# A Fourier layer with a mixture of experts on one core: transposes partly on TensorE, routing by other VectorE steps, first loads on three queues, second products in halves

## The chip, the cores and the metric

The kernel runs on one core of one Trainium2 chip. The metric is the time of one execution in microseconds, as the device reports it; the median of several runs is compared. TensorE (PE) multiplies matrices, VectorE (DVE), ScalarE (ACT) and GpSimd (POOL) work element by element, and SyncE (SP) issues most of the DMA transfers. Every engine takes its instructions in the order in which the program lists them.

## The reference

```python
X = np.fft.rfft(x, axis=1)                      # x: 8 batches x 2496 x 256
Yr = Xr @ w_r - Xi @ w_i + b_r                  # 256 x 256 weights
Yi = Xr @ w_i + Xi @ w_r + b_i
Yr = sign(Yr) * max(abs(Yr) - 0.01, 0); Yi likewise
y = np.fft.irfft(Yr + 1j * Yi, n=2496, axis=1)  # 19968 tokens x 256
logits = y @ w_gate                             # 8 experts
e_idx = argmax(logits); gate_w = softmax(logits)[e_idx]
eom = sigmoid(y @ w_output_gate)
for e in range(8):                              # tokens of expert e
    out[mask] = gate_w * eom[:, e] * (relu(y[mask] @ w1[e]) @ w2[e])   # 256 -> 1024 -> 256
```

## The kernel before, in words

2496 is split as 39 x 64. The transform of a batch goes through these stages, each a set of matmuls on pairs of float16 tiles (a high and a low half of each number, three products for one).

- `load_x` brings a batch's `x` in six tiles; `scales` takes its largest magnitude, by squares on ScalarE or a maximum on VectorE, spreads it over the partitions with a matmul (`allmax`, line 394, whose operand `dg` comes from line 390) and makes the batch's scale `sx` of it.
- `stage1_pair` (line 588) multiplies by the 39-point table; ScalarE (597) and VectorE (598) take the two halves out of PSUM into `at`. There are eight PSUM banks in all.
- `load_a` (613) turns `at` round, 10 pieces `A` a batch of eight blocks of 128 x 128, each piece one transposing DMA on SyncE's queue.
- `stage2` (640) multiplies `A` with the table `ct`; lines 651, 652, 654 and 655 evict the result to `xt`. `mix` (664, 670) applies the weights, lines 685 to 690 the threshold, and line 700 the table `gt`; lines 714 to 717 evict to `bt` and `ste`.
- `inverse` transposes `bt` into `bdt` by DMA (739); `stage4` (765) makes `y`, which goes over `yt` (769) to DRAM as `yd` (785). `logits`, `gate` and `rank` compute each token's expert and its place among the expert's tokens.

Beside this, `weights` turns the expert weights into float16 pairs in DRAM (`wd`).

The tokens are then sorted into tiles of 128 of one expert. `routing` does it twice: phase 0 for the first four batches (64 tiles, placed in pairs), while later batches are still transformed, and phase 1 for all others (99 tiles). `blocks` finds each token's tile; three VectorE steps build, for four columns at a time, 0/1 matrices `ol` and `ob` (1135, 1136) and scale `ob` by the token numbers (1155); the matmul of line 1163 adds them into a map in PSUM; `indices` reads the map out.

For each tile `gathers` fetches the tokens (1236), `tokens` splits and transposes them (1255, 1256, 1269), `up` makes the first products (1354) which are evicted to `hh` (1364, 1365), and `down` the second ones (1325), evicted to `o` (1336) and scattered to the output (1339). `fetch` (1222) loads a tile's expert weights into one of three buffers `wbuf` in two parts, and only where the expert changes.

The order on every engine is set by `Issue`, a planner that runs while the program is built: generators ask for an engine with a due time and a duration, and the earliest due request whose resources are free is taken. The constants at the head of the file are its due times and durations. The first loads stand ahead of it, in the order of the code.

```python
        yield "A", r - SA, 0.66, lambda: A.activation(hi, pv[:, :, :, :m], AF.Copy, scale=sx)
        yield "D", r - SA, 0.68, lambda: V.scalar_tensor_tensor(lo, pv[:, :, :, :m], sx, hi, ALU.mult, ALU.subtract)
```

## Time and profile before

| | |
|---|---|
| median of three runs | 1507.56 us (1501.02 to 1515.1) |
| profiled execution | 1500.14 us, of which the span is 1498.4 us |
| mean granted clock of TensorE | 0.983 |
| busy: TensorE, VectorE, ScalarE, GpSimd | 1420.1, 970.0, 717.4, 590.9 us |
| instructions | 42257 |

The span runs from the first to the last instruction of the program. Busy time of an engine is the time in which at least one of its instructions ran; matmuls overlap each other, and the ends of matmuls are modelled. A line number is that of the listing. The granted clock is a share of 2.4 GHz; a matmul runs at half speed where it is 0.5.

### The profile page before, as it was taken

The numbers are of one execution on the slowest core, as the hardware profiler recorded it, in microseconds if no ns is written. First come the engines' busy times: TensorE is split into PE (matmuls) and PEld (weight loads), VectorE is DVE, ScalarE is ACT, GpSimd is POOL, SyncE is SP. The second block draws the span as 40 slices with busy tenths as digits, with TensorE's granted clock in tenths as the row PEclk, the third lists the DMA queues.
The fourth block names the chain that finished last, engine by engine and source line by source line (L and its number), as shares of the span: only waits on it lengthen the run. The fifth ranks groups of instructions, "written<-read, shape, count | busy, mean of one in ns | idle before, by whom it ended". The sixth has DMA issues, their size and how long they took to land. (4 is left out here: it accounts for less than half of the span.)

```text
span 1498.4 us, 42257 instructions
## 1 busy us (share of the span) xinstructions
PE 1420.1 (95%) x16192; PEld 1280.4 (85%) x16192; DVE 970.0 (65%) x2911; ACT 717.4 (48%) x1386; POOL 590.9 (39%) x664
## 2 busy tenths in 40 slices
PE   4799999998989989999999999999999999999998
PEld 4689887887778867878999988999898989999997
DVE  3677777769988878677777685555454555454532
ACT  4666765767665746343333333433333333333432
POOL 0454535444455545334333324344243333433311
PEclk8799999999999999999999999999999999999999
DMA  8879999999989898988865788765938476477420
GB/s 227 198 164 212 217 225 198 218 221 214 215 209 209 205 223 202 208 241 231 239 185 147 213 227 218 220 208 123 233 80 234 106 208 220 98 235 212 102 51 20
DMA packets 329955, 285.33 MB, mean 190 GB/s; under 512 B 277702, under 2 KB 286536, under 8 KB 317721
## 3 DMA queue, kind: packets, MB, share of 16 engines
q1 hardware_dynamic: 313127, 239.40, 65.4%
q0 software_dynamic: 15648, 42.17, 10.5%
q8 instruction: 127, 2.08, 0.6%
q10 hardware_dynamic: 978, 1.06, 0.3%
q14 instruction: 75, 0.61, 0.1%
HBM read 337.41 MB, written 58.91 MB: 264 GB/s over the span
## 5 line engine op out<-in xcount | busy, mean ns | idle before, releaser
L1354 PE MATMUL ps<-eT,wbuf 128*128 128x128 f16 (+1 forms) x6288 | 451.9, 232 | 5.6 <-DMA wbuf<-wd 4.3
L1325 PE MATMUL ps<-wbuf,hh 128*128 128x256 f16 x3912 | 444.8, 273 | 8.9 <-DVE hh L1365 4.0
L1354 PEld LDWEIGHTS <-wbuf 128*128 128x128 f16 x6288 | 419.7, 98 | 26.0 <-DMA wbuf<-wd 5.2
L1325 PEld LDWEIGHTS <-hh 128*128 128x128 f16 x3912 | 379.5, 98 | 57.0 <-DVE hh L1365 6.5
L1339 POOL DMA_INDIRECT out<-o,sidx x163 | 167.4, 1027 | 494.0 <-ACT o L1336 270.7
L1365 DVE SCALAR_TENSOR_TENSOR hh<-ps,hh 128x512 f16<-128x512 f32 x326 | 220.3, 689 | 206.7 <-ACT hh L1364 195.3
L1364 ACT ACTIVATE hh<-ps 128x512 f16<-128x512 f32 x326 | 188.3, 596 | 194.1 <-PE ps L1354 176.7
L670 PE MATMUL ps<-whl,xt 128*128 128x256 f16 x1920 | 229.3, 276 | 3.8 <-ACT xt L655 1.7
L670 PEld LDWEIGHTS <-xt 128*128 128x128 f16 x1920 | 190.2, 99 | 40.8 <-ACT xt L655 2.5
L1236 POOL DMA_INDIRECT yg<-yd,gidx x163 | 161.2, 989 | 93.2 <-DVE p2e L366 35.4
L1256 DVE SCALAR_TENSOR_TENSOR yhl<-yg,ys,yhl 128x256 f16<-128x256 f32 x163 | 79.6, 488 | 145.1 <-ACT yhl L1255 135.6
L1336 ACT ACTIVATE o<-ps,fac 128x256 f32<-128x256 f32 x163 | 76.8, 471 | 200.0 <-PE ps L1325 168.4
L1255 ACT ACTIVATE yhl<-yg,ys 128x256 f16<-128x256 f32 x163 | 82.2, 505 | 160.6 <-DMA eT<-yhl 78.1
L588 PE MATMUL ps<-f1t,x 117*128 117x120 f32 (+1 forms) x704 | 91.3, 291 | 6.1 <-issue 4.9
L588 PEld LDWEIGHTS ps<-f1t,x 117*128 117x128 f32 (+1 forms) x704 | 88.7, 207 | 7.4 <-issue 5.0
L689 POOL CAST zhl<-z 128x512 f16<-128x512 f32 x44 | 28.4, 647 | 139.1 <-DVE z L686 70.8
L765 PE MATMUL ps<-bdt,f4t 120*117 120x512 f16 x264 | 70.4, 390 | 10.5 <-ACT ste L716 8.5
L700 PE MATMUL ps<-gt,zhl 128*128 128x128 f16 x960 | 65.3, 220 | 9.9 <-DVE zhl L690 3.9
L700 PEld LDWEIGHTS <-zhl 128*128 128x128 f16 x960 | 58.1, 98 | 17.4 <-DVE zhl L690 4.4
L597 ACT ACTIVATE at<-ps,sx 128x480 f16<-128x480 f32 (+1 forms) x88 | 55.3, 649 | 34.2 <-PE ps L588 31.5
L685 ACT ACTIVATE zhl<-ps,sc 128x512 f32<-128x512 f32 x80 | 54.7, 687 | 32.9 <-PE ps L670 28.2
L690 POOL TENSOR_TENSOR zhl<-z,zhl 128x512 f16<-128x512 f32 x51 | 60.6, 1188 | 24.8 <-ACT zhl L688 21.4
(187 smaller groups left out, 1610.5 us busy)
## 6 DMA issues: line engine op xcount, KB each, us to landing
wbuf<-wd SPq DMA_DIRECT2D x262, 1024.0 KB
yd<-yt SPq DMA_DIRECT2D x120, 158.4 KB
x<-in_x SPq DMA_DIRECT2D x120, 156.0 KB
wr<-in_moe_w SPq DMA_DIRECT2D x32, 512.0 KB
wd<-wsp SPq DMA_DIRECT2D x64, 256.0 KB
yg<-yd,gidx POOLq DMA_INDIRECT x163
eT<-yhl SPq DMA_TRANSPOSE x163
out<-o,sidx POOLq DMA_INDIRECT x163
```

What stands on the lines that cost most here:

```text
L588: T.matmul(pv[:, dh, :, m * j:m * j + m], xs[:k, j0 + j, 128 * dh:128 * dh + 128], fw, start=True, stop=True)
L670: T.matmul(yp[:, 256 * j:256 * j + 256], xt_[:, v, 2 * dh + j, 64 - 64 * u:192 - 64 * u], whl[:, dh, vw, 256 * u:256 * u + 256], start=Fal ...
L700: T.matmul(bv[:, j], zhl[:, vz, c:c + 128], gt[:, 2 * p + j, v], start=(n == 0), stop=(n == 2))
L1236: yield "G", r + 5.6 * t - 30, 1.0, lambda: G.indirect_dma_start(out=yg, out_offset=None, in_=src, in_offset=bass.IndirectOffsetOnAxis(ap= ...
L1255: yield "A", r - 10, 0.5, lambda: A.activation(yhl[:, 0], yg[:, :256], AF.Copy, scale=s)
L1256: yield "D", r - 10, 0.48, lambda: V.scalar_tensor_tensor(yhl[:, 1], yg[:, :256], s, yhl[:, 0], ALU.mult, ALU.subtract)
L1325: T.matmul(pt[:, :256], hh[:, v, fc, 128 * n:128 * n + 128], w[:, fc // 2, vw, fc % 2], start=(k == 0), stop=(k == 23))
L1336: yield "A", r - 4, 0.47, lambda: A.activation(o, pt[:, :256], AF.Copy, scale=fac)
L1339: yield "G", r - 4, 1.0, lambda: G.indirect_dma_start(out=out, out_offset=bass.IndirectOffsetOnAxis(ap=sidx[:, t:t + 1], axis=0), in_=o, i ...
L1354: T.matmul(pt[:, 128 * m * j:128 * m * (j + 1)], w[:, dh, g // 4, vw, 128 * (g % 4):128 * (g % 4) + 128], eT[:, :m, v, dh], start=(n == 0) ...
L1364: yield "A", r, 0.6, lambda: A.activation(hv[:, 0], pt, AF.Relu)
L1365: yield "D", r, 0.69, lambda: V.scalar_tensor_tensor(hv[:, 1], pt, 0.0, hv[:, 0], ALU.max, ALU.subtract)
```

## The change

- Six of batch 0's ten `A` pieces, and four of every other batch's, are transposed by matmuls with an identity (`turn_a`) into PSUM and taken from there by ScalarE or VectorE, whichever the planner finds free first.
- `x` of batch 0 is issued by SyncE and ScalarE in turns, the biases and mixing weights by GpSimd; `m16` is loaded in two parts, `ct` and `gt` in two halves each, and what is not needed at once is given to the planner with a later due time.
- Routing: for each column one step over 128 elements makes `ol` and one step with two operations makes the scaled `ob`; the tables are float32 columns, and `ol` and `ob` are stored column by column. `blocks` treats two batches in a step and `indices` four.
- The second products of a tile are made in two halves, each as soon as its part of `hh` is ready, with due times between those of the first products.
- The constants of the planner are other ones; a line or two stands here for all.

```diff
-P = 69.05
-DK = 2.49
+P = 68.49
+TP, TE, QT = 0.56, -1.96, 6.13
+PT = (0, 1, 2, 3, 6, 8), (0, 1, 3, 6)
+DK = 2.8
...
-    for i in range(3):
-        load_x(0, i)
+    for i in range(6):
+        load_x(0, i, (nc.sync, nc.scalar)[i % 2])
...
-    nc.scalar.dma_start(wraw[:, :, 0], w_r.rearrange("(dh p) f -> p dh f", p=128))
+    G.dma_start(wraw[:, :, 0], w_r.rearrange("(dh p) f -> p dh f", p=128))
...
+    def tables_(r):
+
+        for i in range(2):
+            k = slice(K1 // 2 * i, K1 // 2 * (i + 1))
+            n = K1 // 2 * 256
+            yield from move(r, 6.5e5, 0.4, lambda: nc.sync.dma_start(ct[:, k].rearrange("p a b f -> p (a b f)"), cmat[:, n * i:n * (i + 1)]))
+            io.at(io.now + TAIL, io.set, "ct", i)
...
         for p in range(NP):
             yield slots["A"]
             a = st[b, "A", p] = ring(pm, [128, KP, 2, 2, 128], F16, "A", AN)
+            if p in PT[b > 0]:
+                for k in range(KP):
+                    io.go(turn_a(b, p, k, a, r + 2 * DK * p + TP))
+                continue
...
+    def turn_a(b, p, k, a, r):
+
+        def f(i):
+            pt = bank(i)
+            for dh in range(2):
+                for v in range(2):
+                    m = 256 * dh + 128 * v
+                    T.matmul(pt[:, m:m + 128], at[:, KP * p + k, dh, v], eye, start=True, stop=True)
+            return pt.rearrange("p (c v n) -> p c v n", c=2, v=2)
+
+        i, pt = yield "P", r, 0.23, f, True
+        yield [("A", r - TE, 0.58, lambda: A.activation(a[:, k], pt, AF.Copy)),
+               ("D", r - TE + QT, 0.68, lambda: V.tensor_copy(a[:, k], pt))]
...
-                ol = ring(pool, [P3, 128, CB], F16, f"ol{ph}", OL[ph])
-                ob = ring(pool, [P3, n, CB], F16, f"ob{ph}", OL[ph])
...
-                yield "D", r, 0.08 + 0.085 * m, lambda: V.tensor_tensor(ol[:, :, :m], iota[:P3, :, :m], bc(rlo, 128), ALU.is_equal)
-                yield "D", r, 0.08 + 0.066 * m, lambda: V.tensor_tensor(ob[:, :, :m], iota[:P3, :n, :m], bc(blk, n), ALU.is_equal)
+                ol = ring(pool, [P3, CB, 128], F16, f"ol{ph}", OL[ph])
+                ob = ring(pool, [P3, CB, n], F16, f"ob{ph}", OL[ph])
...
+                    for j in range(m):
+                        V.tensor_scalar(ol[:, j], iota[:P3], rlo[:, c0 + j:c0 + j + 1], None, ALU.is_equal)
...
+                    for j in range(m):
+                        V.tensor_scalar(ob[:, j], iota[:P3, :n], blk[:, c0 + j:c0 + j + 1], va[:, c0 + j:c0 + j + 1], ALU.is_equal, ALU.mult)
...
-        yield "D", r, 0.08 + 0.066 * m, lambda: V.tensor_tensor(ob[:, :, :m], ob[:, :, :m], vb, ALU.mult)
...
         for half in range(2 * m):
-            io.go(up(t, m, half, w, eT, ie, hh, r))
-        yield "hh", t
-        yield "w", t, 1
+            io.go(up(t, m, half, w, eT, ie, hh, r + UP * half))
...
-            io.go(down(t + i, m, i, w, hh, ih, r + 4 * m))
+            io.go(down(t + i, m, i, w, hh, ih, r + (5.6 + UP * i) * m + DN))
...
+        for half in range(2):
+            for i in range(m * half, m * half + m):
+                yield "hh", t0, i
+            if half == 0:
+                yield "P", r, 1.31, f, True
+            else:
+                yield "P", r + UP, 1.31, f
```

VectorE at the start, before: `mx` holds a batch's maxima, `x_211` is the first tile of the second batch, line 598 evicts the low halves of the first batch.

```order
L527 TENSOR_SCALAR sc_230<-sxi_240,swi 128x1
L359 TENSOR_REDUCE mx_242<-x_211 117x1
L598 SCALAR_TENSOR_TENSOR at<-ps_164,sx_238,at 128x40x12
L598 SCALAR_TENSOR_TENSOR at<-ps_171,sx_238,at 128x40x12
L598 SCALAR_TENSOR_TENSOR at<-ps_178,sx_238,at 128x40x12
```

The same place now, from the last evictions on (line 628 was 598, line 666 takes a transposed piece from PSUM).

```order
L628 SCALAR_TENSOR_TENSOR at<-ps_270,sx_236,at 128x40x12
L628 SCALAR_TENSOR_TENSOR at<-ps_283,sx_236,at 128x40x12
L491 SCALAR_TENSOR_TENSOR whl<-wr_112,sw,whl 128x2x512
L628 SCALAR_TENSOR_TENSOR at<-ps_290,sx_236,at 128x40x8
L519 MEMSET mx_262 128x12
L666 CAST A_313<-ps_318 128x512
```

The maximum over the second batch's first tile stood before the first eviction; now no maximum of that batch stands among the eleven evictions, and the transposed pieces follow them.

TensorE at the start, before: the last pairs of the first stage, three `allmax` products (of the gate weights and of the second batch), then the second stage.

```order
L588 MATMUL ps_280<-f1t,x_110 128x20x6 x4
L588 MATMUL ps_291<-f1t,x_110 128x20x6 x4
L588 MATMUL ps_299<-f1t,x_114 128x20x4 x4
L394 MATMUL ps_328<-dg_326,one_84 128x128
L394 MATMUL ps_356<-dg_354,one_84 128x128
L394 MATMUL ps_361<-dg_358,one_84 128x128
L640 LDWEIGHTS A_321
```

The same place now; line 661 is the transposing matmul, 32 of which follow before line 696, the second stage.

```order
L618 MATMUL ps_270<-f1t,x_104 128x20x6 x4
L618 MATMUL ps_283<-f1t,x_104 128x20x6 x4
L618 MATMUL ps_290<-f1t,x_108 128x20x4 x4
L661 LDWEIGHTS at
L661 MATMUL ps_318<-t_82,at 128x128
```

The three `allmax` products no longer stand between the two stages; transposing matmuls do.

ScalarE in the expert stage, before: line 1364 evicts half of a tile's first products, line 1336 a tile's second product, line 1255 splits gathered tokens.

```order
L1364 ACTIVATE hh_9453<-ps_25482 128x512
L1364 ACTIVATE hh_9453<-ps_25515 128x512
L1364 ACTIVATE hh_9602<-ps_25544 128x512
L1364 ACTIVATE hh_9602<-ps_25590 128x512
L1336 ACTIVATE o_25684<-ps_25618,fac_24244 128x256
L1255 ACTIVATE yhl_25648<-yg_24992,ys_25654 128x256
L1255 ACTIVATE yhl_25709<-yg_25052,ys_25719 128x256
L1336 ACTIVATE o_25752<-ps_25659,fac_24427 128x256
```

The same now (1458 was 1364, 1340 was 1255, 1430 was 1336).

```order
L1458 ACTIVATE hh_10068<-ps_26117 128x512
L1340 ACTIVATE yhl_26183<-yg_25505,ys_26215 128x256
L1458 ACTIVATE hh_10068<-ps_26186 128x512
L1430 ACTIVATE o_26264<-ps_26167,fac_24840 128x256
L1458 ACTIVATE hh_10068<-ps_26239 128x512
```

Two tiles went through together, four evictions of first products and then two second products; now each tile goes by itself, with one second product between the first products.

## Rows read from the trace of the kernel before

**Rows 1.** Page, busy microseconds of each engine, share of the span, instructions.

```profile
PE 1420.1 (95%) x16192; PEld 1280.4 (85%) x16192; DVE 970.0 (65%) x2911; ACT 717.4 (48%) x1386; POOL 590.9 (39%) x664
```

**Rows 2.** Stretches: length, busy of PE, PEld, DVE, ACT, POOL, clock, DMA share, GB/s.

```profile
0.00:52.00 52.00, 25.47 (x139) 23.50 (x140) 24.45 (x86) 23.62 (x43) 5.64 (x15) 0.75 0.89 224
52.00:350.00 298.00, 288.75 (x3214) 255.34 (x3213) 214.02 (x511) 199.44 (x379) 144.59 (x178) 0.99 0.96 206
350.00:600.00 250.00, 228.45 (x2473) 193.64 (x2471) 215.38 (x607) 161.40 (x321) 126.81 (x156) 0.97 0.93 211
600.00:700.00 100.00, 97.36 (x920) 83.70 (x919) 71.72 (x283) 38.90 (x78) 35.79 (x40) 1.00 0.93 232
700.00:950.00 250.00, 248.93 (x2320) 224.59 (x2318) 176.38 (x599) 93.69 (x180) 88.95 (x87) 1.00 0.73 209
950.00:1470.00 520.00, 509.96 (x6855) 479.76 (x6853) 262.53 (x820) 193.21 (x375) 184.19 (x184) 1.00 0.60 160
```

**Rows 3.** Waits of TensorE, 0 to 52 us: total, times, longest.

```profile
PE ps L394 <- DVE dg L390: 20.3, 5, 9.5
```

**Rows 4.** Timeline of the start: start us, us, engine, line [idle before, releaser].

```profile
29.66 1.22 DVE L359 TENSOR_REDUCE mx<-x 117x1 f32<-117x1024 f32 x1 [5.69 <-DMA x<-in_x]
...
31.61 5.38 PE L588 MATMUL ps<-f1t,x 117*128 117x120 f32 x24 [4.86 <-issue]
...
39.94 1.36 SPq L613 DMA_TRANSPOSE A<-at  x1
...
45.68 1.49 PE L640 MATMUL ps<-ct,A 128*128 128x128 f16 x12
...
46.55 9.83 SPq L613 DMA_TRANSPOSE A<-at  x6
...
51.97 0.63 PE L664 MATMUL ps<-b,t 128*128 128x512 f16 x1
```

**Rows 5.** Waits of TensorE, VectorE and ScalarE, 52 to 700 us.

```profile
PE ps L765 <- ACT ste L716: 8.5, 4, 2.9
...
DVE mx L359 <- DMA x<-in_x: 19.2, 11, 4.2
...
ACT yt L769 <- DMA yd<-yt: 11.9, 3, 6.8
...
ACT bt L714 <- DMA bdt<-bt: 7.7, 1, 7.7
```

**Rows 6.** Stretches, columns as in rows 2, around lower clock.

```profile
234.00:238.00 4.00, 3.91 (x20) 2.79 (x21) 2.87 (x7) 1.29 (x3) 2.26 (x4) 0.57 0.88 236
...
528.00:535.00 7.00, 6.12 (x41) 3.88 (x39) 5.56 (x18) 1.77 (x4) 0.95 (x1) 0.52 1.27 162
```

**Rows 7.** Groups of instructions: busy us, mean ns; and one line's ns min/median/max.

```profile
L1354 PE MATMUL ps<-eT,wbuf 128*128 128x128 f16 x4752 | 274.7, 219 | 4.6 <-DMA wbuf<-wd 4.3 <-issue 0.2
...
L652 DVE SCALAR_TENSOR_TENSOR xt<-ps,xt x80: 668/681/693, 47.8 to 571.4; 128x512 f16<-128x512 f32 x80
```

**Rows 8.** Timeline of TensorE around a group of four map matmuls.

```profile
807.12 0.54 PE L1163 MATMUL ps<-ob,ol 117*128 117x99 f16 x4
807.49 4.77 PE L1325 MATMUL ps<-wbuf,hh 128*128 128x256 f16 x42
```

**Rows 9.** Groups of VectorE, then two lines' ns min/median/max.

```profile
L1135 DVE TENSOR_TENSOR ol<-t,rlo 117x512 f16<-117x512 f16 x72 | 33.1, 460 | 0.0
...
L1136 DVE TENSOR_TENSOR ob<-t,blk 117x396 f16<-117x396 f16 (+1 forms) x72 | 27.4, 380 | 0.0
L1155 DVE TENSOR_TENSOR ob<-ob,t 117x396 f16<-117x396 f16 (+1 forms) x72 | 27.0, 375 | 0.6
...
L654 DVE TENSOR_SCALAR xt<-xt x32: 273/289/1159, 89.4 to 535.5; 128x512 f16<-128x512 f16 x32
...
L1135 DVE TENSOR_TENSOR ol<-t,rlo x72: 281/417/1397, 399.1 to 867.0; 117x512 f16<-117x512 f16 x60, 117x256 f16<-117x256 f16 x12
```

**Rows 10.** Waits of TensorE from 700 us on: total, times, longest.

```profile
PE ps L1354 <- DMA wbuf<-wd: 4.3, 4, 1.4
```

More of the change, by code (lines that the diff above doesn't have):

```diff
@@ L116 @@
 ORDERED = {ET.PE, ET.Activation, ET.DVE, ET.Pool, ET.SP}
-P = 69.05
-DK = 2.49
-T1 = 0.95
-S2 = 4.88
-E1 = 57.1
-DS = 3.58
-ES = 24.32
-Z1 = 7.79
-Z2 = 7.98
-IV = 28.52
-IS = 2.16
-GO = -51.32
-R0 = 1.64
-R1, G1 = 0.0, 0.9
-GA = 1.22
-W0 = 31.63
-W1 = 30.72
+P = 68.49
+TP, TE, QT = 0.56, -1.96, 6.13
+PT = (0, 1, 2, 3, 6, 8), (0, 1, 3, 6)
+DK = 2.8
+T1 = 0.91
+S2 = 12.79
+E1 = 52.83
+DS = 2.64
+ES = 26.59
+Z1 = 8.23
+Z2 = 6.78
+IV = 17.09
+IS = 2.48
+GO = -51.84
+R0 = 4.49
+R1, G1 = 0.0, 0.8
+GA = 1.36
+W0 = 37.0
+W1 = 30.58
+TG = 28.27
+HEAD = 15.0
 LAG = dict(P=0.17, A=0.16, D=0.14, G=0.09, S=0.0)
@@ L1082, in indices @@
         cs = slice(T_A * ph, T_A * ph + n)
-        acc = scratch()[:, :2 * n].rearrange("p (v n) -> p v n", v=2)
-        two = scratch()
-        m, w = two[:, :n], two[:, n:2 * n]
-        V.memset(acc, 0.0)
-        for i in range(nb):
-            mp = route["map", ph, i // per][1][:, n * (i % per):n * (i % per) + n]
-            V.tensor_copy(m, mp)
-            V.tensor_scalar(w, m, 0.0, float(S * i + S // 2 + 1), ALU.not_equal, ALU.mult)
-            yield
-            V.tensor_tensor(acc[:, 0], acc[:, 0], w, ALU.add)
-            V.tensor_scalar(w, m, 0.0, None, ALU.is_gt)
-            yield
-            V.tensor_tensor(m, m, w, ALU.subtract)
-            V.tensor_tensor(acc[:, 0], acc[:, 0], m, ALU.add)
-            yield
@@ L1098, in indices, with total @@
-        V.tensor_scalar(gidx[:, cs], acc[:, 0], -1.0, 0.0, ALU.add, ALU.max)
-        V.tensor_scalar(acc[:, 1], acc[:, 0], 0.0, float(1 << 20), ALU.is_equal, ALU.mult)
-        V.scalar_tensor_tensor(sidx[:, cs], acc[:, 0], -1.0, acc[:, 1], ALU.add, ALU.add)
+        acc = psm.tile([128, 2 * T_B], F32, tag="gL", name="gL", bufs=1).bitcast(F16)[:, :4 * n].rearrange("p (r n) -> p r n", r=4)
+        def total(dst, src, c):
+            with nc.allow_low_precision(reason="integers up to 1248, one a slot"):
+                V.tensor_reduce(dst, src.rearrange("p (b n) -> p n b", b=c), AX.X, ALU.add)
@@ new lines, in indices @@
+        rounds = [(i, min(4, nb - i, per - i % per)) for i in range(nb) if i % per in range(0, per, 4)]
+        for k, (i, c) in enumerate(rounds):
+            mp = route["map", ph, i // per][1][:, n * (i % per):n * (i % per + c)]
+            two = lambda a: a.rearrange("p (b n) -> p b n", b=c)
+            m, w = (scratch16()[:, :c * n] for _ in range(2))
+            r = 2 * min(k, 1)
+            V.tensor_copy(m, mp)
+            yield
+            V.scalar_tensor_tensor(two(w), two(m), 0.0, iota[:, 1 + i:1 + i + c].rearrange("p (b o) -> p b o", o=1).broadcast_to([128, c, n]), ALU.not_equal, ALU.mult)
+            yield
+            total(acc[:, r], w, c)
+            yield
+            V.scalar_tensor_tensor(w, m, 0.0, m, ALU.is_gt, ALU.subtract)
+            yield
+            total(acc[:, r + 1], w, c)
+            if k:
+                V.tensor_tensor(acc[:, :2], acc[:, :2], acc[:, 2:], ALU.add)
+            yield
@@ L1122, in routing @@
             yield "tiles", 0
-        for b in range(nb):
-            yield from parts(blocks(ph, b), "D", r, 0.55)
+        for b in range(0, nb, 2):
+            yield from parts(blocks(ph, b, min(2, nb - b)), "D", r, 0.5)
         io.set("blocks", ph)
@@ L1141, in routing @@
             yield 1.0
-        yield from parts(indices(ph), "D", r, 0.48)
+        yield from parts(indices(ph), "D", r, 0.6)
         io.set("ix", ph)
@@ L1162, in f @@
             for j in range(m):
[L1163 removed]
+                T.matmul(route[key][1][:, n * i:n * i + n], ol[:, j], ob[:, j], start=(q + j == 0), stop=(q + j == NQ - 1))
         if q == 0 and i == 0:
@@ L1366, in up @@
         io.free(i)
-        st["nh", t] += 1
-        if st["nh", t] == 2 * m:
-            io.set("hh", t)
+        io.set("hh", t, half)
     def blocks_(r):
@@ L1374, in blocks_ @@
             io.go(block(k, r + 5.6 * t))
+    io.busy["S"] = HEAD
     io.go(setup(-60))
+    io.go(tables_(-60))
     io.go(load())
```

185 lines of the change are left out of this document (111 added, 74 removed).

## The prediction

> **What bounds the kernel now.** I read the shares of busy time first: TensorE is busy 95% of the span [rows 1], so time can only come out of what TensorE does or out of its idle time. Then the table by stage [rows 2], which says where that idle time lies: 26.5 us of the first 52 us, 9.3 of the next 298, 21.6 of the 250 from 350 to 600, 2.6 up to 700, and then little: 1.1 of 250 and 10.0 of 520 us. So the expert stage, 60% of the run, is full of matmuls, and the Fourier stage and the start are where something is to be had. In the same table VectorE is 86% busy between 350 and 600 (215.4 of 250), and the DMA engines have a share of 0.93 to 0.96 from 52 to 700 us.
>
> The waits of TensorE come next. At the start it stands 20.3 us for the `dg` steps of VectorE [rows 3], and the timeline says why [rows 4]: VectorE stands 5.69 us before a maximum over the second batch's `x`, and behind it in its queue are the second halves of the first batch's evictions, which free the PSUM banks; TensorE resumes at 31.6. The first transpose by DMA is issued at 39.94 (all of `at` is ready then), the first product of the next stage starts at 45.68 and the first mixing product at 51.97. Between 52 and 700 us no single wait is large (8.5 us is the largest line), but VectorE and ScalarE themselves wait for late DMAs: 19.2, 11.9 and 7.7 us [rows 5]. What an idle stretch costs is more than itself: four times in 230 to 535 us the granted clock is at the lower level, 1.2 GHz; the first and the last of the four stretches are shown [rows 6]. Two are like the first ((1 - 0.57) x 4 x 2 = 3.4 us at half speed) and two like the last (6.7 us): 20 us, of which half, 10 us, is lost.
>
> **The change, part by part.**
>
> *Transposes by TensorE.* 34 of the 80 `A` transposes (6 of batch 0, 4 of each other one) leave the DMA queue and become 34 x 2 x 4 = 272 matmuls of 128 columns. Such a matmul takes 274.7/4752 = 58 ns of TensorE [rows 7]. Of the 48 of batch 0, 32 stand before the first product of the next stage, in a stretch that was idle; 240 x 58 ns = 13.9 us are added to a full engine. They also add 68 evictions of 512 columns. 39 of these stand on VectorE, at 0.681 us [rows 7] 26.6 us; about 15 of them, 10 us, fall into 350 to 600. From the queue goes 34 x 1.64 us (9.83 us for six in a row, [rows 4]) = 56 us, a tenth of the DMA time of 52 to 600 us.
>
> *The start.* The loads are split over three queues and 0.3 MB less lies ahead of the last piece of `x`, worth 1.3 us at the 224 GB/s of the first row of rows 2; but ScalarE now issues eight loads before its first squares, so I give this nothing. The order of VectorE at the start puts the second batch's maxima behind all evictions: the 5.7 us stall goes, and `at` is ready at about 34 instead of 39.9. From there to the first product passed 5.7 us; now it is 32 matmuls at the low clock, 32 x 0.116 = 3.7 us, and TensorE has no `dg` product of the second batch ahead of them: 2 us less. From first product to first mixing product 6.3 us passed, 5.2 without the DMA waits: 1 us less. With the transposes of the next pieces already done I expect the first mixing product 9 to 15 us earlier, at 37 to 43; I take 12. What is late next is VectorE, which has 11 evictions, then five of the new ones. Bounds: 0 (the second batch's `x`, now behind half of `ct` and other tables, holds the pipeline up later) and -15.
>
> *Waits from 52 to 700 us.* Idle time plus lower clock are 33.4 + 10 = 43 us. The DMA relief of 56 us works on the late `x`, `yt` and `bdt` transfers. VectorE gets no relief worth counting between 350 and 600: the column steps stay about even (below), the blocks and indices lose some 100 of 168 steps, which at 0.375 us [rows 9] and with the rest two to four times as wide is some 20 us, 7 of them here, against the 10 us of new evictions. I take -12, under a third. Bounds: -43, and +20, as the new evictions stand in the same in-order queues and TensorE waits for them.
>
> *Column steps.* Per four columns three wide steps become four of 128 and four of 64 or 99 columns. Removed are 33.1 + 27.4 + 27.0 = 87.5 us; added 528 steps. A one-source f16 step of 512 columns takes 273 ns at least [rows 9], so one of 128 costs between a quarter of it and all of it: 36 to 144 us. Taken: 0.15 us each, 79 us, no change. VectorE in 700 to 950 is 71% busy and hides either end.
>
> *Map matmuls.* Their operands now lie contiguously. Four of them hold TensorE from 807.12 to 807.49, 92 ns each, for 99 columns [rows 8]; at the 58 ns per 128 columns of rows 7 they would take 42 to 45. 176 x 50 ns = 8.8 us, all of it on the full engine between 600 and 950. Bounds 0 and -11.
> The Trainium skill speaks against this term: SBUF — State Buffer, section "Door 1: The DMA port swizzle", in its note on cachelines, says that 16-bit data may be read with a stride of up to 8 elements for free, and the stride was 4. By it the gain would be nil. The trace shows the 92 ns and not which operand makes it, so I keep the term and give the rule a chance below.
>
> *Second products in halves.* The same matmuls; only the order changes, from two tiles' first products and then two second ones to alternating halves. TensorE's idle time here is 10 us in 520, 4.3 of it for weights [rows 10], so at most -9. A weight buffer's first half was free for 4 or 6 tile halves of 2.7 us before its next use (10.8 or 16 us); now it is always 9 quarter steps of 1.35 us, 12 us. At an expert change three buffers of 2 MB come in, 6.3 MB or 28 us at 224 GB/s, against 12 + 3 x 5.4 = 28 us. I take 0, with -9 and +25.
>
> *Sum.* 1498.4 + 13.9 - 12 - 12 - 8.8 + 0 = 1479.5 us of span; 1.7 us lie around it (1500.14 - 1498.4), so 1481.2 us in the profiled execution. The median shown is 1507.56, 0.495% over that execution; I carry the ratio over: 1488.5 us, 1.3% less.
>
> **The rivals.**
> 1. *The earlier start is eaten.* DMA share 0.93 to 0.96 says that the queues set the pace of the Fourier stage, and 26 us of idle time at the start are then only moved: start 0, waits 0, so 1498.4 + 13.9 - 8.8 + 1.7 = 1505.2, as a median 1512.7. For it: the late transfers of rows 5. Against it: 56 us less in the queue, and TensorE 97% busy from 52 to 350. Chance 0.17.
> 2. *Map matmuls keep 92 ns,* all else as forecast: 1488.5 + 8.8 = 1497. Chance 0.10.
> 3. *The narrow steps clog VectorE in 350 to 600.* The one-source step that has a floor of 273 ns reaches 1159, and the wide one with 281 reaches 1397 [rows 9]: some steps stand for close to a microsecond. With 176 narrow steps here instead of 72, VectorE at 86% could gain 15 us, and the waits grow by 15 instead of falling by 12: 1488.5 + 27 = 1516. The floor that most steps keep, 281 against a median of 417, speaks against a full effect. Chance 0.08.
> The Trainium skill states such a rule in SBUF — State Buffer, section Terms: a VectorE step on two ports and a GpSimd step exclude each other for the whole step. The trace agrees, by 273 against 1159 ns.
> 4. *Weights come late at expert changes* (slower than before). The margin reckoned above is zero. At a tenth less DMA rate each of the seven changes waits 2.8 us and more, and after a wait of that length the clock was at its lower level for 3.4 us or more [rows 6], 1.7 us lost: 7 x (3.6 + 1.7) = 37 us, 1525.6. It decides from 2.7 us per change, where the gain is gone. Against it: the waits of before are only 1.4 us at the longest [rows 10] with 10.8 us of lead in the worse case, which grows. Chance 0.08.
>
> **How the numbers follow.** The forecast has the remaining chance, 0.57, with a range of its own from 1474 to 1502. About 1% is what a measurement of this kernel can tell from no change: 1492.5 and 1522.6 are the bounds. Of the forecast 0.50 lies below 1492.5, and 0.05 comes from case 2 with a better start: faster 0.55. Slower are case 4 and a little of case 3 and 1: 0.08. The rest, 0.37, is within 1%. The range reaches from a start of -15 with two thirds of the waits gone (1464) to between cases 3 and 4 (1514).
>
> **What would show it.** Right: the first mixing product at 37 to 43 us; 272 new matmuls of 55 to 60 ns; map matmuls at 42 to 50 ns from start to start; idle time of TensorE from 52 to 700 us under 30 us and fewer than four stretches at the lower clock; from 950 to 1470 us idle time between 5 and 15 us. Wrong: if VectorE's waits for `x` and ScalarE's for `yd` stay as long, the DMA relief was not what was missing; if TensorE waits for `ol` or `ob` in 350 to 600, case 3; if the waits for `wbuf` exceed 15 us, case 4.

## The result and the profile after

The changed kernel took 1489.71 us (median of 4 runs, 1479.56 to 1491.88) beside 1505.81 for the kernel before on the same chip: ratio 0.9865, 95% interval [0.9829, 0.99]. Six runs of a later series gave 1489.61 us and 0.9866 [0.9835, 0.9898]. So it is 1.3% faster. The profiled execution of the first series took 1490.97 us, with a span of 1489.1 and a mean granted clock of 0.986.

The busy shares of the page answer to [rows 1]:

```profile
PE 1425.2 (96%) x16464; PEld 1288.6 (87%) x16464; DVE 1023.4 (69%) x3167; ACT 738.7 (50%) x1415; POOL 582.0 (39%) x659
```

A ledger of the span can be made from this one row and the spans: TensorE's busy time rose by 5.1 us (1420.1 to 1425.2), its idle time fell by 14.4 (1498.4 - 1420.1 = 78.3 to 1489.1 - 1425.2 = 63.9), and the difference is the 9.3 us of the spans. Where the idle time changed stands in the table by stage (columns as in [rows 2]: length, busy time of PE, PEld, DVE, ACT and POOL, clock, DMA share, GB/s):

```profile
0.00:52.00 52.00, 34.21 (x281) 32.63 (x282) 27.04 (x79) 27.33 (x49) 9.43 (x19) 0.87 0.85 206
52.00:350.00 298.00, 295.51 (x3393) 264.17 (x3392) 241.68 (x587) 224.22 (x426) 150.15 (x186) 1.00 0.85 206
350.00:600.00 250.00, 232.67 (x2589) 198.47 (x2587) 230.22 (x678) 157.88 (x307) 118.83 (x147) 0.98 0.77 189
600.00:700.00 100.00, 98.33 (x906) 84.93 (x905) 82.33 (x335) 39.88 (x79) 35.30 (x41) 1.00 0.88 233
700.00:950.00 250.00, 249.51 (x2464) 225.25 (x2463) 188.18 (x709) 96.10 (x185) 92.38 (x94) 1.00 0.71 217
950.00:1455.00 505.00, 485.42 (x6454) 455.45 (x6454) 246.48 (x774) 183.99 (x355) 169.02 (x170) 0.98 0.58 156
```

Beside [rows 2], the idle time of TensorE is now 17.8 us instead of 26.5 up to 52 us, 2.5 instead of 9.3 up to 350, 17.3 instead of 21.6 up to 600, 1.7 instead of 2.6 up to 700. It went up in the last row: 505 - 485.4 = 19.6 us, where the kernel before has 10.0 in 520. The clock fell there too, from 1.00 to 0.98. The DMA share fell from 0.96 to 0.85 and from 0.93 to 0.77. VectorE's busy time from 350 to 600 us rose from 215.4 to 230.2 of 250.

The start, as in [rows 4] (start, duration, engine, line; the last bracket is the idle time before and what ended it):

```profile
1.80 13.64 ACTq L324 DMA_DIRECT2D x<-in_x  x8
15.47 1.28 ACT L343 ACT_TABLE_LOAD   x1 [15.47 <-DMA x<-in_x]
...
34.97 3.49 PE L661 MATMUL ps<-t,at 128*128 128x128 f16 x31 [1.36 <-DVE mx L519]
...
38.25 3.27 PE L696 MATMUL ps<-ct,A 128*128 128x128 f16 x36
...
41.73 0.38 PE L720 MATMUL ps<-b,t 128*128 128x512 f16 x1
...
44.57 0.61 PE L661 MATMUL ps<-t,at 128*128 128x128 f16 x8
45.01 0.83 PE L696 MATMUL ps<-ct,A 128*128 128x128 f16 x12
```

The transposes stand where the DMA transposes stood, and the first mixing product (L720, L664 before) comes at 41.73 us instead of 51.97. A transposing matmul takes 106 ns from start to start in the group of 31 (34.97 to 38.25 us, granted clock 0.50) and 55 ns in the later group of eight (44.57 to 45.01, granted clock 1.00). New is that ScalarE does nothing until 15.47 us: its queue issues eight loads until then.

Of ScalarE's waits in [rows 5], that for `yd` fell from 11.9 to 6.5 us, 6.1 of it in one wait, and that for `bdt`, 7.7 before, is gone. Three more waits: the two of TensorE that the prediction named as alarms, then VectorE's wait for `x`, 19.2 us before:

```profile
PE ps L1248 <- DVE ob L1221: 7.1, 11, 1.6
...
PE ps L1448 <- DMA wbuf<-wd: 18.1, 8, 3.2
...
DVE mx L382 <- DMA x<-in_x: 6.6, 5, 2.6
```

And the narrow column steps and the map matmuls, which answer to [rows 9] and [rows 8]; the timeline pair shows four map matmuls from 791.30 to the next matmul at 791.49, 48 ns each:

```profile
L1217 DVE TENSOR_SCALAR ol<-t,rlo 117x128 f16<-117x128 f16 x264 | 57.2, 286 | 0.0
L1221 DVE TENSOR_SCALAR ob<-t,blk,va 117x99 f16<-117x99 f16 x176 | 43.1, 311 | 0.0
L1221 DVE TENSOR_SCALAR ob<-t,blk,va 117x64 f16<-117x64 f16 x88 | 28.7, 388 | 0.0
...
791.30 0.35 PE L1248 MATMUL ps<-ob,ol 117*128 117x99 f16 x4
791.49 1.47 PE L1448 MATMUL ps<-eT,wbuf 128*128 128x256 f16 x12
```

What an expert change costs now, as one wait in the timeline and as a stretch of the table around another one: 9 us at a mean clock of 0.81 are (1 - 0.81) x 9 x 2 = 3.4 us at the lower level.

```profile
997.14 1.51 PE L1448 MATMUL ps<-eT,wbuf 128*128 128x128 f16 x24 [2.71 <-DMA wbuf<-wd]
...
1060.00:1069.00 9.00, 6.71 (x71) 5.63 (x69) 3.43 (x11) 2.35 (x5) 2.49 (x3) 0.81 0.93 235
```

### The profile page after: what moved, and what is told of

Read it like the earlier page. It is cut to its first block, busy times and chain, and to the rows that moved or that the text cites. A ratio compares the mean times of both kernels' runs of the same rounds, so it can differ in the third digit from the quotient of the medians.

```text
span 1489.1 us, 42875 instructions
## 1 busy us (share of the span) xinstructions
PE 1425.2 (96%) x16464; PEld 1288.6 (87%) x16464; DVE 1023.4 (69%) x3167; ACT 738.7 (50%) x1415; POOL 582.0 (39%) x659
## 5 line engine op out<-in xcount | busy, mean ns | idle before, releaser
L1448 PE MATMUL ps<-eT,wbuf 128*128 128x128 f16 (+1 forms) x6288 | 485.0, 233 | 18.3 <-DMA wbuf<-wd 18.1
L1413 PE MATMUL ps<-wbuf,hh 128*128 128x256 f16 x3912 | 482.1, 275 | 1.9 <-issue 1.9
L1448 PEld LDWEIGHTS <-wbuf 128*128 128x128 f16 x6288 | 432.2, 98 | 44.3 <-DMA wbuf<-wd 20.9
L1459 DVE SCALAR_TENSOR_TENSOR hh<-ps,hh 128x512 f16<-128x512 f32 x326 | 224.8, 690 | 250.3 <-ACT hh L1458 201.8
L1458 ACT ACTIVATE hh<-ps 128x512 f16<-128x512 f32 x326 | 193.5, 594 | 296.3 <-PE ps L1448 277.2
L1433 POOL DMA_INDIRECT out<-o,sidx x163 | 164.2, 1007 | 304.8 <-ACT o L1430 111.4
L746 POOL TENSOR_TENSOR zhl<-z,zhl 128x512 f16<-128x512 f32 x62 | 73.0, 1179 | 56.5 <-ACT zhl L744 52.4
L1221 DVE TENSOR_SCALAR ob<-t,blk,va 117x99 f16<-117x99 f16 (+1 forms) x264 | 71.7, 337 | 0.0
```

Of the source, the lines that this page charges most:

```text
L1413: T.matmul(st["pt", t][1][:, :256], hh[:, v, fc, 128 * n:128 * n + 128], w[:, fc // 2, vw, fc % 2], start=(half == k == 0), stop=(half == ...
L1433: yield "G", r - DN, 1.0, lambda: G.indirect_dma_start(out=out, out_offset=bass.IndirectOffsetOnAxis(ap=sidx[:, t:t + 1], axis=0), in_=o, ...
L1448: T.matmul(pt[:, 128 * m * j:128 * m * (j + 1)], w[:, dh, g // 4, vw, 128 * (g % 4):128 * (g % 4) + 128], eT[:, :m, v, dh], start=(n == 0) ...
L1458: yield "A", r, 0.6, lambda: A.activation(hv[:, 0], pt, AF.Relu)
L1459: yield "D", r, 0.69, lambda: V.scalar_tensor_tensor(hv[:, 1], pt, 0.0, hv[:, 0], ALU.max, ALU.subtract)
```

## The experiments

All ratios are to the kernel before, timed in the same series on the same chip.

**Is the new order of the second products to blame for the weight waits?** Four kernels, with two theories. A: the weight buffers are freed later. B: the order is innocent.

The order of before in the changed kernel:

```diff
-            io.go(up(t, m, half, w, eT, ie, hh, r + UP * half))
+            io.go(up(t, m, half, w, eT, ie, hh, r))
+        yield "hh", t
...
-            io.go(down(t + i, m, i, w, hh, ih, r + (5.6 + UP * i) * m + DN))
+            io.go(down(t + i, m, i, w, hh, ih, r + 4 * m))
...
-        for half in range(2):
...
+        i, pt = yield "P", r, 2.61, f, True
```

> The changed kernel with the second products in the order of before again (two tiles' first products, then two whole second products); all else of the change stays. Theory A (the new order frees the weight buffers later, so the weights are late at the expert changes): TensorE's waits for wbuf from its second-products line fall from 18.1 us to about 4, as before, idle time from 950 us to the end of the stage falls from 19.6 to about 10 us, no stretch at the lower clock stays there, and the time falls by 15 to 20 us, to about 1472 (ratio to before 0.975). Theory B (the order is innocent, the weights are late because of something else in the change, such as the stage that now begins earlier or what else the queue carries): the waits stay between 14 and 20 us and the time within 5 us of 1490 (ratio 0.984 to 0.990).

Measured: 1490.35 us, 0.9876 [0.9824, 0.9928]. The waits of TensorE from 930 us on (total, times, longest), and the stages from 950 and from 600:

```profile
PE ps L1410 <- ACT hh L1449: 6.0, 6, 2.1
PE ps L1439 <- issue: 2.9, 11, 0.4
PE ps L1439 <- DMA wbuf<-wd: 2.7, 4, 1.4
PE ps L1410 <- DVE hh L1450: 1.9, 6, 0.3
...
950.00:1455.00 505.00, 490.49 (x6581) 458.61 (x6579) 251.29 (x785) 186.12 (x360) 175.28 (x176) 1.00 0.59 157
600.00:700.00 100.00, 94.21 (x829) 79.52 (x828) 76.91 (x309) 38.56 (x77) 33.59 (x39) 1.00 0.85 223
```

Theory A is right about the mechanism: the weight waits fall from 18.1 to 2.7 us. It is wrong about the price: the ratio, 0.9876 beside 0.9865, doesn't move beyond its interval of half a per cent, and the 15 to 20 us expected are out. In this order TensorE waits 7.9 us for the activations `hh` that the second products read, and between 600 and 700 us it is idle for 5.8 us instead of 1.7. Idle time from 950 to 1455 and from 600 to 700 us together: 14.5 + 5.8 = 20.3 us, against 19.6 + 1.7 = 21.3 in the changed kernel. One order waits for weights, the other for activations. The lower clock is not in these sums: from 950 to 1455 us it costs the changed kernel 8.5 us (5.1 in its second profile) and this one 1.7. By idle time and clock together this order should have gained 4 to 8 us, about what the interval can hide; whether it did stays open.

Later and earlier second products (the planner's offsets of first and second products):

```diff
-UP, DN = 2.8, 1.4
+UP, DN = 0.0, 1.4
```

> The changed kernel with one number changed so that each second product comes two quarter steps (2.7 us) later against the first products of the following tiles, so that a weight buffer's second part comes free 2.7 us later. Theory A: each of the seven expert changes waits up to 2.7 us longer for each tile that goes through it; the waits for wbuf rise from 18.1 us to 30 or more, and the time by 12 to 35 us, to 1502 to 1525. Theory B: the waits and the time stay as in the changed kernel, within 5 us of 1490.

```diff
-UP, DN = 2.8, 1.4
+UP, DN = 0.0, -2.0
```

> The changed kernel with two numbers changed so that each second product is as early as its inputs allow (one half right behind the next tile's first half-product), and a weight buffer's second part comes free two quarter steps (2.7 us) earlier than in the changed kernel. Theory A: the waits for wbuf fall from 18.1 us to under 6, the stretches at the lower clock in the expert stage go, and the time falls by 12 to 18 us, to 1472 to 1478. Theory B: within 5 us of 1490. A third outcome: the second products now wait for ob the activations of their own tile (hh from ScalarE and VectorE), since they come only one half-product behind it; then the waits for hh rise by over 5 us and the gain is given back.

Measured: 1505.43 us, 0.9971 [0.9943, 0.9999] for the later ones, 1510.58 us, 1.0 [0.9965, 1.0034] for the earlier ones. The waits from 930 us on, the first row of the later, the other two of the earlier:

```profile
PE ps L1448 <- DMA wbuf<-wd: 25.7, 16, 2.9
```

```profile
PE ps L1413 <- ACT hh L1458: 14.3, 13, 2.4
PE ps L1413 <- DVE hh L1459: 4.0, 13, 0.3
```

With later second products the weight waits rise as theory A has it, from 18.1 to 25.7 us and from 8 to 16 waits, somewhat less than the 30 expected; the time rises by 16, of which the 7.6 us of longer weight waits are only a half, and the rest is not explained. With earlier ones the weight waits are gone from the list altogether, but the third outcome came, and dearer than expected: 18.3 us of waits for `hh`, and a kernel 21 us slower than the changed one. TensorE is also idle for 14.2 us between 600 and 950 us, where the changed kernel has 2.2. The changed kernel, with a distance between these two, is the best of the three.

The new order alone, in the kernel before:

```diff
+UP, DN = 2.8, 1.4
...
+            io.go(up(t, m, half, w, eT, ie, hh, r + UP * half))
...
+            io.go(down(t + i, m, i, w, hh, ih, r + (5.6 + UP * i) * m + DN))
```

> The kernel before with nothing changed but the order of the second products (in halves between first products, as in the changed kernel). Theory A: the waits for wbuf rise from 4.3 us to 15 to 20, with stretches at the lower clock behind some of them, and the time rises by 12 to 20 us over before, to about 1523 (ratio 1.008 to 1.013). Theory B: within 5 us of before. The view of the prediction, that this part is worth nothing, is theory B's number too.

Measured: 1515.45 us beside 1511.77, ratio 1.0029 [0.9998, 1.0059], and the weight waits (4.3 in [rows 10]):

```profile
PE ps L1364 <- DMA wbuf<-wd: 15.1, 10, 2.7
```

Again the mechanism is theory A's and the price is nearly theory B's: by the interval, the part costs between nothing and 9 us by itself.

**What are the transposes by TensorE worth?** The changed kernel ran once more in this series as the standard.

> The changed kernel itself once more, beside the next three kernels and as often as they, so that parts worth less than one per cent can be told. Expected as before: 1490 us, ratio to the kernel before 0.983 to 0.990.

It took 1489.61 us, as given above.

```diff
-PT = (0, 1, 2, 3, 6, 8), (0, 1, 3, 6)
+PT = (), ()
```

> The changed kernel with all 80 transposes of A by DMA again: 272 matmuls of 56 ns (15 us of TensorE, some 13 of it on the full engine) and 68 evictions (39 of them on VectorE, 26 us) go, 56 us come back into the DMA queue; all else of the change stays. Theory C (the relief of the queue pays for the transposes' work on TensorE): the DMA share from 52 to 350 us rises from 0.85 to about 0.95, VectorE waits for x 15 to 20 us instead of 6.6, the first mixing product comes 2 to 5 us later, TensorE's idle time from 52 to 600 us rises from 20 to 30 us or more with stretches at the lower clock, and the time is 1493 to 1502 (ratio 0.988 to 0.994). Theory D (the shorter waits came from the other parts of the change, the order of VectorE's steps and the loads): the waits stay as in the changed kernel, TensorE saves its 13 us, and the time is about 1477 (ratio 0.977).

Measured: 1534.71 us, 1.0149 [1.011, 1.0189]. The table by stage:

```profile
52.00:350.00 298.00, 280.15 (x3141) 247.34 (x3139) 216.79 (x550) 201.81 (x387) 144.40 (x179) 1.00 0.95 214
350.00:600.00 250.00, 215.60 (x2280) 180.91 (x2279) 202.13 (x563) 147.67 (x286) 116.32 (x145) 0.95 0.80 185
```

Theory D's time is out. Theory C has the direction and the DMA share (0.95), but undoing this part costs 45 us where it expected 3 to 12: TensorE is idle for 17.9 + 34.4 = 52.3 us from 52 to 600 us, and the clock of 0.95 in the second row, instead of 0.98, takes more. Two of C's signs didn't come. The first mixing product starts at 39.91 us, no later than in the changed kernel (41.73 and 39.68 us in its two profiles), though behind one piece's 12 products instead of 36. And VectorE's wait for `x` is not back at 15 to 20 us but shorter still:

```profile
DVE mx L382 <- DMA x<-in_x: 3.6, 3, 1.4
```

ScalarE, though, waits 8.5 us for `x` (1.1 in the changed kernel, 6.4 before) and 12.4 us for `yd` (6.5 and 11.9). So the relief of the queue shows in ScalarE's waits; the early first mixing product and VectorE's short wait come without it, as theory D had it. Only a part of TensorE's idle time is a wait for the transposes themselves (`PE ps L696 <- DMA A<-at`: 5.7 us up to 350, 2.8 up to 600); the rest is spread over waits for VectorE and ScalarE. That could be a misfit: the planner's numbers go with the change. So the same again with 21 more lines of the planner's constants as they were before:

```diff
-P = 68.49
+P = 69.05
...
-DK = 2.8
...
-S2 = 12.79
+DK = 2.49
...
+S2 = 4.88
...
-XL, TA, TB, YS, WL, WS = -59.47, -28.73, -9.58, -1.01, -12.61, -8.79
+XL, TA, TB, YS, WL, WS = -65.09, -25.41, -10.06, 3.95, 0.18, -20.21
```

> The last run but two (all transposes of A by DMA) with 22 of the planner's spacing numbers set to those of the kernel before (the period, the spacing of the pieces, the leads of the stages, the due times of loads), which belong to a plan with all transposes in the queue. That run took 1534.7 us, 45 more than the changed kernel and 24 more than the kernel before, with TensorE idle for 52 of 548 us from 52 to 600. Theory G (most of the 45 us is a misfit of the numbers to the queue, not the queue itself): the idle time from 52 to 600 us falls to 25 to 40 us and the time to 1495 to 1515; what is left over the changed kernel's 1489.6 is what the transposes by TensorE are worth. Theory H (the queue itself sets that price in the changed kernel's order of steps): idle time stays over 45 us and the time over 1520.

Measured: 1528.67 us, 1.0123 [1.0101, 1.0145].

```profile
52.00:350.00 298.00, 285.00 (x3182) 251.92 (x3180) 220.71 (x566) 199.52 (x386) 145.56 (x183) 0.99 1.00 220
350.00:600.00 250.00, 218.90 (x2268) 180.65 (x2268) 204.15 (x577) 147.21 (x289) 118.22 (x147) 0.92 0.81 193
```

The idle time is 13.0 + 31.1 = 44.1 us, a hair under theory H's bound, and the time above it: these numbers were worth some 6 us and not the 45. The clock from 350 to 600 us is lower again, 0.92, 40 us at the lower level against 27 in the run before and 10 in the changed kernel. Half of that is lost, so in these two profiles the clock takes back what the idle time gains. With these numbers the DMA share from 52 to 350 us reaches 1.00. So without the transposes by TensorE the rest of the change is slower than the kernel before by 18 to 23 us; with them it is 22 faster. The parts don't add up one by one. How much of the difference is the queue and how much the numbers that were not set back stays open.

**Do the narrow column steps hold VectorE up?**

```diff
-                    for j in range(m):
-                        V.tensor_scalar(ol[:, j], iota[:P3], rlo[:, c0 + j:c0 + j + 1], None, ALU.is_equal)
+                    V.tensor_tensor(ol[:, :, :m], iota[:P3, :, :m], bc(rlo, 128), ALU.is_equal)
...
-                    for j in range(m):
-                        V.tensor_scalar(ob[:, j], iota[:P3, :n], blk[:, c0 + j:c0 + j + 1], va[:, c0 + j:c0 + j + 1], ALU.is_equal, ALU.mult)
+                    V.tensor_tensor(ob[:, :, :m], iota[:P3, :n, :m], bc(blk, n), ALU.is_equal)
+                    V.tensor_tensor(ob[:, :, :m], ob[:, :, :m], bc(va, n), ALU.mult)
```

> The changed kernel with the three wide, column-interleaved steps for four columns of before instead of four of 128 and four of 64 or 99 columns, in the same places of the order; all else of the change stays. Theory E (the narrow steps, with 129 us instead of 88, hold VectorE up from 350 to 600 us): VectorE's busy time there falls from 230 to about 215 us, TensorE's waits of the map matmuls for ob (7.1 us) fall under 2, the map matmuls go back to 92 ns (8 us more, nearly all from 600 to 950 us), and the sum is 1484 to 1493, within 6 us of the changed kernel. Theory F (these waits come from where the steps stand in VectorE's order, not from their length): the waits stay over 5 us, only the 8 us of slower map matmuls show, and the time is about 1498.

Measured: 1486.88 us, 0.9845 [0.9818, 0.9873].

```profile
350.00:600.00 250.00, 236.57 (x2679) 205.16 (x2678) 219.60 (x601) 163.59 (x317) 125.73 (x151) 0.99 0.87 199
...
PE ps L1248 <- DVE ob L1221: 3.9, 5, 1.9
...
795.99 0.53 PE L1248 MATMUL ps<-ob,ol 117*128 117x99 f16 x4
796.34 1.49 PE L1448 MATMUL ps<-eT,wbuf 128*128 128x256 f16 x12
```

This is theory E, nearly as it stands: VectorE is 10 us less busy from 350 to 600 us, TensorE idle for 13.4 us there instead of 17.3 (19.9 in the standard's profile), and the map matmuls are back at 350/4 = 88 ns. The wait for `ob` falls to 3.9 us and not under 2. Gain and loss about cancel: the two parts of the change that belong together, narrow steps and contiguous map operands, are together worth nothing that these runs can tell.

**Which operand made the map matmuls slow?**

```diff
-                ob = ring(pool, [P3, CB, n], F16, f"ob{ph}", OL[ph])
+                ob = ring(pool, [P3, n, CB], F16, f"ob{ph}", OL[ph]).rearrange("p n c -> p c n")
```

> The changed kernel with the moving operand of the map matmuls, ob, laid out with a stride of 4 elements again, ol contiguous as it is. One look at the map matmuls from start to start in the expert stage, 48 ns in the changed kernel and 92 before. If the moving operand makes the difference: 85 to 95 ns. If the stationary operand makes it: 45 to 50 ns. The rule of the Trainium skill in SBUF — State Buffer, section Door 1: The DMA port swizzle, that a stride of up to 8 elements of 16 bits costs nothing when read, would by itself give 45 to 50 ns here and in the counterpart. The time within 8 us of the changed kernel's.

It ran once, in 1494.96 us. Four map matmuls from 797.82 to 798.17:

```profile
797.82 0.53 PE L1248 MATMUL ps<-ob,ol 117*128 117x99 f16 x4
798.17 2.80 PE L1448 MATMUL ps<-eT,wbuf 128*128 128x256 f16 x24
```

88 ns with only the moving operand strided. The counterpart, with the wide steps but the comparison writing `ob` contiguously by columns, so that `ol` alone is strided:

```diff
-                ob = ring(pool, [P3, n, CB], F16, f"ob{ph}", OL[ph])
+                ob = ring(pool, [P3, CB, n], F16, f"ob{ph}", OL[ph])
...
-                    V.tensor_tensor(ob[:, :, :m], iota[:P3, :n, :m], bc(blk, n), ALU.is_equal)
-                    V.tensor_tensor(ob[:, :, :m], ob[:, :, :m], bc(va, n), ALU.mult)
+                    V.tensor_tensor(ob.rearrange("p c n -> p n c")[:, :, :m], iota[:P3, :n, :m], bc(blk, n), ALU.is_equal)
+                    V.tensor_tensor(ob[:, :m], ob[:, :m], va[:, cs].rearrange("p (c o) -> p c o", o=1).broadcast_to([P3, m, n]), ALU.mult)
```

> The run with wide column steps once more, but ob laid out contiguously: the comparison writes it with a stride, the product by the values goes over contiguous columns; ol stays interleaved with a stride of 4. If the moving operand alone makes the 92 ns of the map matmuls (as the run with only ob strided says, 91 ns), they take 45 to 50 ns here although the stationary operand is strided; if the stationary one also counts, 70 to 92. The comparison with strided writes costs 0 to 0.3 us more than the 0.27 us floor of the wide steps, the product likewise. With cheap steps: VectorE as busy from 350 to 600 us as with the wide steps (about 220 us), 8 us of TensorE's work less between 600 and 950, so 1479 to 1483; with steps of 0.5 us or more each: VectorE back at 230 us, 1487 to 1492.

Measured: 1550.21 us, 1.0243 [1.0217, 1.027]. The map matmuls, and the comparison here:

```profile
791.74 0.35 PE L1248 MATMUL ps<-ob,ol 117*128 117x99 f16 x4 [1.46 <-DVE ob L1221]
791.93 2.78 PE L1413 MATMUL ps<-wbuf,hh 128*128 128x256 f16 x24
...
L1220 DVE TENSOR_TENSOR ob<-t,blk 117x396 f16<-117x396 f16 x40 | 80.8, 2020 | 0.0
```

The same step in the run with wide steps:

```profile
L1220 DVE TENSOR_TENSOR ob<-t,blk 117x396 f16<-117x396 f16 x40 | 14.3, 357 | 0.0
```

190/4 = 48 ns with a strided stationary operand: the moving operand alone counts. As a version this one failed, by 60 us over the changed kernel, for a reason outside the expected range: the comparison with strided writes takes 2.02 us instead of 0.357, not up to 0.3 us more.

**Does ScalarE's queue hold the start up?**

```diff
-        load_x(0, i, (nc.sync, nc.scalar)[i % 2])
+        load_x(0, i, nc.sync)
```

> The changed kernel with the first batch's x loads all on SyncE's queue, so that ScalarE doesn't issue any of them before its squares (in the changed kernel it issues eight from 1.80 to 15.44 us and begins its squares at about 16.7). If ScalarE's queue is what makes the start late: its first step comes at 12 to 14 us instead of 15.47, the squares' sum is ready 2 to 3 us earlier and the first mixing product comes at 38 to 40 us instead of 41.7; the time falls by 2 to 4 us. If the last loads of x bound it: the loads land later through one queue, ScalarE waits for them instead, and the first mixing product comes at 41 to 45 us; time unchanged or up to 3 us longer.

Measured: 1486.25 us, 0.9836 [0.9812, 0.986].

```profile
0.74 13.42 SPq L324 DMA_DIRECT2D x<-in_x  x17
1.80 1.28 ACT L343 ACT_TABLE_LOAD   x1 [1.80 <-issue]
...
10.30 1.06 ACT L524 ACTIVATE junk<-x 117x1024 bf16<-117x1024 f32 x1 [7.00 <-DVE mx L519]
...
38.53 0.38 PE L720 MATMUL ps<-b,t 128*128 128x512 f16 x1
```

17 loads are issued through one queue in about the time that nine took beside eight on ScalarE's (13.42 us against 13.31 and, in the second profile of the changed kernel, 11.76), the first square starts at 10.30 us (16.88 in the changed kernel, 15.38 in its second profile), and the first mixing product comes 3.2 us earlier than in the first profile of the changed kernel, though only 1.1 earlier than in its second (39.68). The first answer is right about the mixing product (38 to 40 us) and about the size, while ScalarE's first step came far earlier than its 12 to 14 us, at 1.80; the interval of the time overlaps that of the changed kernel, so the 3 us are seen in the start and not shown in the total.

**What the runs point to.** Wide steps where VectorE is the fullest, narrow ones into contiguous columns where TensorE is, `ol` wide throughout, and the loads of the last run:

```diff
+                    if ph:
+                        for j in range(m):
+                            V.tensor_scalar(ob[:, j], line[:P3, :n], sc[:, 0, c0 + j:c0 + j + 1], sc[:, 1, c0 + j:c0 + j + 1], ALU.is_equal, ALU.mult)
+                        return
                     V.tensor_tensor(ob[:, :, :m], iota[:P3, :n, :m], bc(blk, n), ALU.is_equal)
                     V.tensor_tensor(ob[:, :, :m], ob[:, :, :m], bc(va, n), ALU.mult)
...
-        load_x(0, i, (nc.sync, nc.scalar)[i % 2])
+        load_x(0, i, nc.sync)
```

> What the runs point to, put together: wide column steps (ol and, in the first routing phase of 350 to 600 us where VectorE is the fullest, ob too), but in the second phase, from 600 to 900 us, where TensorE is full and VectorE isn't, ob by narrow steps into contiguous columns (with the two scalars copied to fp32 once per two batches), so that the moving operand of the 99-column map matmuls is contiguous; and the first x loads all on SyncE's queue. From the run with wide steps (1486.9): 176 x 44 ns = 8 us less on TensorE between 600 and 950, and 3 us from the loads: 1476 if they add up. If the narrow steps make VectorE late in the second phase too, or the saved TensorE time is given back at the expert changes as the pair order's gain was, 1480 to 1487.

Measured: 1477.79 us (1469.69 to 1481.46), ratio 0.9793 [0.9761, 0.9825], which doesn't touch the interval of the changed kernel, [0.9835, 0.9898].

```profile
350.00:600.00 250.00, 236.75 (x2632) 204.42 (x2633) 214.49 (x596) 161.37 (x314) 120.99 (x146) 0.97 0.85 199
...
791.20 0.35 PE L1264 MATMUL ps<-ob,ol 117*128 117x99 f16 x4
791.39 1.47 PE L1429 MATMUL ps<-wbuf,hh 128*128 128x256 f16 x12
...
PE ps L1464 <- DMA wbuf<-wd: 17.8, 9, 3.0
```

It has VectorE at 214.5 us from 350 to 600, TensorE idle for 13.2 there, the map matmuls at 48 ns, and the 17.8 us of weight waits are still there. It came out 1.8 us from the 1476 of the sum; by ratio, since this series ran on another chip, the sum is 0.9765 and the distance 4 us. Against the run with wide steps alone, [0.9818, 0.9873], the intervals still touch.

## Why the prediction was right, point by point

The forecast was 1488.5 us, a ratio of 0.9874; measured were 0.9865 and 0.9866. That it is this close is luck. In its own terms the sum was further off: a span of 1479.5 was reckoned, and the two profiles of the changed kernel have 1489.1 and 1485.1. The median of before was carried over at 0.495% above its profiled execution, while the profiled executions of the changed kernel lie within 0.2% of its medians; the 6 to 10 us of the one and the 7 of the other cancelled. What the sum lacked is the expert stage, which has 18 us more of idle time and lower clock than before (15 in the second profile) where the sum had 0; what it had too small is the stretch from 52 to 700 us.

- *Transposes by TensorE, +13.9.* 240 matmuls at 56 ns from start to start are 13.4 us, right by its direct cost. That the rest of the change costs 45 us more without them, the sum with its -12 for the waits didn't contain.
- *Start, -12.* The first mixing product came at 41.73 and 39.68 us, 10 to 12 earlier, inside the 37 to 43 given. Most of it is the earlier `at` (34.9 us instead of 39.9, as reckoned). The transposing matmuls bring the first product of the next stage to 3.3 us behind it, as the working had it, against 4.9 with all transposes in the queue; but the first mixing product comes as early there (39.91 and 39.36 us), since one piece goes ahead of it instead of three. The term "I give this nothing" for ScalarE's eight loads before its first squares was mis-sized: the loads cost 1 to 3 us of the start.
- *Waits from 52 to 700 us, -12.* Idle time fell from 33.4 to 21.5 us, -11.9 (-9.1 in the second profile). "Fewer than four stretches at the lower clock" holds: there are three, at 436, 497 and 528 us, of 3.4 us each, where there were some 20 us before, and that makes some 5 us more. All three stand right behind waits of the map matmuls, of 0.65 to 1.59 us. The mechanism, the relief of the DMA queue, is only in part the one claimed. ScalarE's waits bear it out, as said above; VectorE's wait for `x`, 19.2 us before and 6.6 now, does not, since it is 3.6 and 9.2 us in the two kernels with all transposes in the queue. What shortened it, the order of VectorE's steps, the due times of the loads or another part, was not tried.
- *Column steps, 0.* This is the step that failed in size: "0.15 us each, 79 us". They kept VectorE busy for 57.2 + 43.1 + 28.7 = 129 us, near the upper bound of 144. One of 128 columns took 234 ns at least and 248 in the median; the floor of 273 ns of the wide one-source step was the nearer row, and the middle was taken instead. That put some 10 of the 15 us more on VectorE from 350 to 600 us, as the wide steps show, and made about half of the wait of 7.1 us for `ob`: rival 3's mechanism at a small part of its price. The wide steps took 4 to 6.5 us of idle time away. Rival 3 judged by "281 against a median of 417" that most steps keep the floor; but 281 ns is a step of 256 elements, and those of 512 took 410 at least, so most did keep theirs.
- *Map matmuls, -8.8.* 92 to 48 ns for 176 of them is -7.7 us. Rival 2 and the rule that would have kept the 92 ns are out. The Trainium skill, SBUF — State Buffer, section "Door 1: The DMA port swizzle", lets 16-bit data be strided by 8 elements for free; for a moving operand strided by 4 the runs show 88 ns against 48, for a stationary one they agree with the page (48 ns).
- *Second products in halves, 0.* This is right in sum and wrong in the margin. "Margin zero" at the expert changes was not zero: all seven waited, 1.8 to 3.2 us, 18.1 us in all with an eighth wait of 0.5, above the 15 us that the prediction set as the sign of rival 4; the idle time from 950 to 1470 us is 19.6 us and not 5 to 15. Of the five stretches of 3.4 us at the lower clock in that stage four stand behind such a wait. That is 9.5 us more idle time than before and 8.5 us lost at half speed, half the 37 us of rival 4. Yet the runs put the part at -1 and +4 us, each with an interval of some us, and the order of before has its own waits, for `hh`. The prediction saw that order only in a profile with 10 us of idle time; in the changed kernel it has 14.5, and 4 more at 600 to 700 us. That the part comes out near 0 is thus not for the reason given.
- *Rival 1*, the start eaten by the queues: out for the changed kernel, since the DMA share fell to 0.85 and 0.77 and the idle time with it. The two kernels with all transposes in the queue start as early and end 18 to 23 us behind the kernel before, which is its mechanism, with the misfit of the numbers in it.
- *The range.* Its ends don't follow from their own terms: a start of -15 and two thirds of the 43 us of waits give 1469 and not 1464, and 1514 lies between cases 1 and 3, not 3 and 4.

## What to carry to other kernels

A wait that a change makes is priced against the wait that the alternative makes, not against none: here the weight waits of 18 us were real, and the kernel without them had 18 us of waits for activations and was 21 us slower. Give each stage the form that spares its own full engine, as the last version does with one computation built in two ways, rather than one form everywhere. And where a change was planned as a whole, taking one part out measures that part and the misfit of all others: undoing a part worth 14 us of direct cost cost 45.

## What the runs showed of the hardware

- A matmul whose fp16 moving operand is read with a stride of 4 elements ran at about half rate: 88 to 92 ns instead of 48 for 99 columns. The stationary operand with the same stride costs nothing that the starts show (48 ns).
- A VectorE step of 396 fp16 elements that writes successive elements 99 elements apart took 2020 ns against 357 with contiguous writes, 5.1 against 0.9 ns per element. For 256 elements 64 apart it was 1377 ns, 5.4 per element.
- At these widths width hardly counts: VectorE steps with one fp16 source took 234 ns at least and 248 in the median for 128 columns, 273 and 289 for 512 [rows 9]. The steps of `ob` with two operations took 305 ns in the median for 99 columns and 294 for 64. The means of 286 ns for 128 columns and 388 for 64 are higher because some steps take up to 1.25 us, and those stand beside GpSimd: all 24 steps of over 0.6 us among the 528 overlap a GpSimd step. The four steps shown would take 1.0 us at the median:

```profile
483.78 1.74 DVE L1217 TENSOR_SCALAR ol<-t,rlo 117x128 f16<-117x128 f16 x4
...
483.99 1.16 POOL L746 TENSOR_TENSOR zhl<-z,zhl 128x512 f16<-128x512 f32 x1
```

- ScalarE did no work while its queue issued DMA loads: eight of them held it from 1.80 to 15.44 us, and without them it began at 1.80. Putting them on SyncE's queue made that queue hardly longer (17 in 13.42 us, nine in 11.76 and 13.31).
